# Batch 0's plain q and k loaded as fp32 over two other queues, half the warm-up matmuls, and the output in eleven tiles

## The chip, the core and the metric

One core of a Trainium2 chip runs the kernel. A core has TensorE (PE; its weight loads are shown as PEld), VectorE (DVE), ScalarE (ACT), GpSimd (POOL), a sync engine (SP) and 16 DMA engines. The metric is the device time of one execution in microseconds (us). A second number, the span, runs from the first to the last instruction in the profile of one execution; the time is a little longer than the span. DMAs are issued by SP, ACT or POOL, each through a queue of its own; here a DMA that casts fp32 to fp16 on its way is issued by POOL.

## The reference

The program is windowed attention followed by a soft mixture of experts:

```python
q, k, v: (8, 8, 576, 64) fp32                      # batch, heads, rows, width
scores = q @ k.T / 8
mask: heads 0-3 "plain":   0 <= i - j < 32
      heads 4-7 "dilated": 0 <= i - j < 128 and (i - j) % 4 == 0
x = softmax(masked scores) @ v                     # -> (4608, 512)
logits = x @ phi                                   # phi (512, 32): 8 experts x 4 slots
slot_input = softmax(logits, over rows).T @ x      # (32, 512)
slot_out[e] = relu(slot_input[e] @ w1[e]) @ w2[e]  # w1 (8, 512, 1024), w2 (8, 1024, 512)
out = softmax(logits, over slots) @ slot_out       # (4608, 512) fp32
```

The inputs are 28.3 MB of q, k and v and 33.6 MB of expert weights, all fp32; the output is 9.4 MB.

## The kernel before

**Homes.** SBUF holds eight tiles `home0` to `home7` (all line numbers below are those of the kernel before). `load_batch(b)` fills home b with the fp16 copies of batch b: `qp`, `kp` (plain heads 0 to 3, 96 partitions x 4 heads x 6 rows), `vp`, `vt` (v of the plain heads, and the last 64 rows of all heads), `qd`, `kd` (dilated heads) and `vd`. All are casting DMAs on POOL's queue, issued in program order at L160 (v), L182 (q and k) and, for batch 0 alone, L185. When a batch is used up, `load_w1` (L237) and `load_w2` (L248, L251) put the weights of expert b into the same home, again on POOL's queue. POOL's order is fixed by hand (`manual_schedule`): all 56 loads of the eight batches, then the 17 weight loads; each weight load waits until its home is free.

**Batch 0.** SP first loads heads 0 and 1 of q in fp32 into a tile of its own, `q0` (L76), and then the identity `ident` (L80), the band mask `mask` (L81) and `phi_sb` (L82). A DVE copy casts `q0` into home 0 (L179). POOL loads the plain k of batch 0 first (L182), then heads 2 and 3 of its q (L185), then v.

**Start of the engines.** DVE begins with 25 fills of constants (L104 to L131), ahead of the cast at L179. PE begins with `warm(6, ...)`: 24 matmuls of `ident` by itself (L549), whose result nothing reads, and then the transposes of unit 0.

**Attention.** A unit is one pair of heads of one batch; 32 units run in the order plain, dilated, plain, dilated within a batch. `transposes` (L273, L288) turns q and k on PE, with copies out at L278 and L293; `select_v` gathers rows of v with matmuls (L203, L214, L223), copied out by ACT at L211 and L232; `scores`, `softmax_parts`, `values` and `x_transposes` follow; `front_logits`, `front_rows` and `front_slots` do the mixture's first half one batch behind. `front_rows` also sums, for every output row, the slot weights, and keeps their reciprocals in `rrow`, one column for each set of 128 output rows (L469).

**Experts and output.** `expert_in` (L667, L675, L678) and `expert_out` (L691) run over the eight experts. The last weight load is that of `w2[7]`, in two halves (L251): the last eight matmuls at L691 need them. ACT copies the sum out as `so` (L708). The output loop then takes 18 tiles of 256 rows: two matmuls of 128 rows each (L729), one scaled out of PSUM by ACT (L731) and one by DVE (L733) into one of six buffers `ot`, and one DMA of 512 KB on SP's queue (L739). A partition holds two neighbouring rows, 4 KB that lie together in the output. Tile 0 is done in four half-width matmuls, and two DMAs of 256 KB (L737).

Of the kernel before, what the change touches and what calls it, by code (L numbers as in the profile page):

```python
# [9 lines left out]
FP32 = mybir.dt.float32  # L10
# [5 lines left out]
B = 8  # L16
H = 8
S = 576
D = 64
# [5 lines left out]
N_ROWS = B * S  # L25
DMODEL = H * D
# [6 lines left out]
QW = 160  # L33
RP, NP = 6, 96
RD, ND = 12, 48
CL = S // DIL
DW = CL + 16
NU = 4 * B
NV = 2

# [14 lines left out]
def kernel(  # L55
# [10 lines left out]
    nc = tc.nc  # L66
# [17 lines left out]
    keep = ctx.enter_context(tc.tile_pool(name="keep", bufs=1))  # L84

# [14 lines left out]
    phi4 = kept([128, 4, 4, N_SLOTS], "phi4")  # L100
    U_sb = kept([128, DMODEL], "U_sb", FP32)

    for b in range(1, B + 1):
        nc.vector.memset(ET[:, S * b : S * b + 64], 0.0)  # L104
    nc.vector.memset(quarter, 0.25)
    nc.vector.memset(quarters, 0.25)
    nc.vector.memset(ones, 1.0)
    nc.vector.memset(xT[:, :, S:], 0.0)
    nc.vector.memset(pick, 0.0)
    nc.vector.memset(phi_by, 0.0)  # L110

    Pp = kept([128, 2, NKB, 256], "Pp")
    P1 = kept([128, 2, 4, 128], "P1")
# [8 lines left out]
    nc.vector.memset(Pp[:, :, :, QW:], 0.0)  # L122

    nc.vector.memset(Pp[:, :, 4, 64:QW], 0.0)
    nc.vector.memset(Pp[0:1, :, 4, 64:128], 1.0)
    nc.vector.memset(P2, 0.0)
    nc.vector.memset(P2[0:1, :, :, 0, 16:32], 1.0)
    for i in range(2):
        nc.vector.memset(vd[i][:, :, D : D + 1], 1.0)
    for i in range(NV):  # L130
        nc.vector.memset(vp[i][:, :, :, D : D + 1], 1.0)  # L131

    hTp = [kept([128, 8, 60], f"hTp{e}") for e in range(4)]

# [13 lines left out]
    ps_s = tc.alloc_tile_pool(name="ps_s", bufs=2, space=bass.MemoryType.PSUM)  # L148

    raws, w_tiles = {}, {}  # L150

    def load_batch(b):
        t = homes[b]
        parts = {}
        at = 0

        def load_v(nm, h0, n_h, r0, dst):
            n_p = dst.shape[0]
            dst = dst.rearrange("p (h x) -> p h x", h=n_h)
# [99 lines left out]
    def transposes(u):  # L259
        b, hp = unit(u)  # L260
        for nm in ("q", "k"):
            if nm == "q":
                dst = qT_pool.tile([128, S], FP16, name=f"qT{u}", tag="qT")
                qTs[u] = dst
            else:
                dst = kTp if hp < 2 else kTd
                kTs[u] = dst
            if hp < 2:
                raw = raws[b][nm + "p"]
                rg = ring.tile([128, RP, NP], FP16, name=f"rg{nm}{u}", tag="ring")  # L270
                for r in range(RP):
                    for h in range(2):
                        nc.tensor.transpose(  # L273
                            rg[64 * h : 64 * h + 64, r, :],
                            raw[:, 2 * hp + h, D * r : D * r + D],
                            ident[0:NP, 0:NP],
                        )
                nc.scalar.copy(  # L278
                    out=dst[:, 0:S].rearrange("c (p r) -> c p r", r=RP),
                    in_=rg.rearrange("c r p -> c p r"),  # L280
                )
            else:
                raw = raws[b][nm + "d"]
                rg = ring.tile([128, 3, 4, ND], FP16, name=f"rg{nm}{u}", tag="ring")
                for a in range(3):
                    for cc in range(2):
                        j = 2 * a + cc
                        nc.tensor.transpose(  # L288
                            rg[:, a, 2 * cc : 2 * cc + 2, :].rearrange("c h p -> c (h p)"),
                            raw[:, hp - 2, 128 * j : 128 * j + 128],  # L290
                            ident[0:NP, 0:NP],
                        )
                (nc.scalar.copy if nm == "q" else nc.vector.tensor_copy)(  # L293
                    out=dst[:, 0:S].rearrange("c (g p a) -> c g p a", g=4, a=3),
                    in_=rg.rearrange("c a g p -> c g p a"),
                )

    def scores(u):
        b, hp = unit(u)
# [159 lines left out]

    def front_rows(b):  # L460
        r0 = b * S
        t0, t1 = r0 // 256, (r0 + S) // 256
# [4 lines left out]
        for n in range(2 * (t1 - t0)):  # L467
            c0 = 256 * t0 + 256 * (n // 2) + n % 2
            nc.tensor.matmul(  # L469
                ep[:, 10, n : n + 1], ET[:, c0 : c0 + 255 : 2], quarter, start=True, stop=True  # L470
            )
        nc.vector.reciprocal(out=rrow[:, 2 * t0 : 2 * t1], in_=ep[:, 10, 0 : 2 * (t1 - t0)])

    def front_slots(b):
        up = ring.tile([128, DMODEL], FP32, name=f"u{b}", tag="ring")
# [123 lines left out]
    select_v(0)  # L599
    st = scores(0)  # L600
    softmax_parts(0, st)
    transposes(2)
    for u in range(NU + 5):
# [9 lines left out]
        if 0 <= b < B:  # L613
            if ph == 1:
                if b == B - 1:
                    last_logits(lr, 3)
                    last_slots(last, lr)
                front_logits(b)
            elif ph == 2:
                front_rows(b)  # L620
            elif ph == 3 and b < B - 1:
                front_slots(b)
        if u == 1:
            spread_phi()
        if u == NU:
# [88 lines left out]

    ps_f = tc.alloc_tile_pool(name="ps_f", bufs=3, space=bass.MemoryType.PSUM)
    out_pool = ctx.enter_context(tc.tile_pool(name="outp", bufs=1))
    ots = [out_pool.tile([128, 2, DMODEL], FP32, name=f"ot{i}", tag=f"out{i}") for i in range(6)]
    for t in range(N_ROWS // 256):
        ot = ots[t % 6]
        rows = out[256 * t : 256 * t + 256, :].rearrange("(m j) d -> m j d", j=2)  # L720
        for j in range(2):
            cols = ET[:, 256 * t + j : 256 * t + j + 255 : 2]
            scale = rrow[:, 2 * t + j : 2 * t + j + 1]
            halves = ((0, 256), (256, 512)) if t == 0 else ((0, 512),)
            for n, (d0, d1) in enumerate(halves):
                n = j if t else n
                fp = ps_f.tile([128, DMODEL], FP32, name=f"f{t}_{j}{n}", tag=f"f{n}")
                fp = fp[:, 0 : d1 - d0]
                nc.tensor.matmul(fp, cols, so[:, d0:d1], start=True, stop=True)  # L729
# [6 lines left out]
            if t == 0:  # L736
                nc.sync.dma_start(out=rows[:, j], in_=ot[:, j])  # L737
        if t > 0:
            nc.sync.dma_start(  # L739
                out=rows.rearrange("m j d -> m (j d)"), in_=ot.rearrange("m j d -> m (j d)")  # L740
            )
    ps_f.release()

# [29 lines left out]
```

## Time and profile before

| what | before |
|---|---|
| time, median of 3 runs | 185.99 us (185.93 to 188.54) |
| time of the profiled execution | 186.0 us |
| its span | 184.2 us |
| busy: PE, DVE, ACT, POOL | 147.0, 117.1, 116.5, 48.3 us |
| read from HBM, written | 62.02 MB, 9.44 MB |
| POOL's queue: packets, MB written | 22480, 30.79 |
| SP's queue: packets, MB written | 3376, 9.89 |
| SP's first issues: `q0`, `ident`, `mask`, `phi_sb` | 0.74, 1.16, 1.65, 2.12 us |
| POOL's first issues: k, q, v | 1.29, 2.09, 2.73 us |
| warm-up matmuls | 24, from 4.05 us, 3.47 us |
| first output DMA issued | 158.72 us |

How to read it: the row of slices in the profile gives the busy share of each engine in 40 equal parts of the span. GB/s counts what DMA engines wrote, so a cast of fp32 to fp16 counts half of what it reads, and a plain fp32 copy counts all of it. The DMA share is packet time over the time of 16 engines; packets overlap, so it can be over 1. A table by stretch gives busy time of each engine, the granted clock of TensorE, the DMA share and the rate for any stretch of the span. The chain of waits follows back from the last instruction to what released each piece of work.

### The profile page before, as it was taken

What the parts mean: (1) busy time and instruction counts of PE and PEld (TensorE: products, weight loads), DVE (VectorE), ACT (ScalarE), POOL (GpSimd) and SP (SyncE); (2) the same over time, 40 slices, a digit from 0 to 9 for tenths busy, and PEclk for the clock granted to TensorE, in tenths of its full rate; (3) what the DMA queues carried; (4) which work ended last, traced back from release to release, by engine and by line L of the source; (5) the groups of instructions that cost most, each with busy time, mean ns of one, the idle gap of its engine ahead of it and who ended that gap; (6) DMA issues with size and microseconds to landing.
All of it is one profiled execution on the core that took longest, in us unless ns stands there. A gap on an engine that the chain in (4) does not pass through costs nothing.

```text
span 184.2 us, 6078 instructions
## 1 busy us (share of the span) xinstructions
PE 147.0 (80%) x2595; PEld 101.0 (55%) x2595; DVE 117.1 (64%) x363; ACT 116.5 (63%) x208; POOL 48.3 (26%) x77
## 2 busy tenths in 40 slices
PE   1879889699899899979978989989698983895300
PEld 1647666566676667757666667667585330331000
DVE  7605995948778788797786877869801110595610
ACT  2248879677888797798789698878131220785510
POOL 7754545455554545410011010022000000000000
PEclk9999999979999999999999999999965798589755
DMA  5999999999999999999999999999999994399995
GB/s 106 190 202 204 200 202 203 202 201 204 200 203 200 204 201 206 215 211 221 205 223 210 222 206 218 213 216 221 210 222 213 209 212 87 128 422 418 421 418 245
DMA packets 25883, 41.06 MB, mean 223 GB/s; under 512 B 1792, under 2 KB 20352, under 8 KB 24832
## 3 DMA queue, kind: packets, MB, share of 16 engines
q0 software_dynamic: 22480, 30.79, 94.4%
q1 hardware_dynamic: 3376, 9.89, 13.6%
q8 instruction: 20, 0.33, 0.6%
q14 instruction: 7, 0.06, 0.1%
HBM read 62.02 MB, written 9.44 MB: 388 GB/s over the span
## 4 chain that ended last, share of the span: by engine, by line
DMA 54%; PE 15%; issue 14%; ACT 5%; DVE 4%; POOL 4%; ACTq 0%; POOLq 0%
DMA home<-in_moe_w_dram 32%; DMA home<-in_q_dram 6%; DMA home<-in_k_dram 6%; DMA out_dram<-ot 5%; DMA home<-in_v_dram 5%; PE f L729 3%; PE l L434 2%; ACT pd L342 2%; PE sel L203 2%; PE rgx L414 1%; PE o L393 1%; PE rgq L273 1%; POOL home L182 1%; DVE P L351 1%; ACT qT L278 1%
## 5 line engine op out<-in xcount | busy, mean ns | idle before, releaser
L398 DVE TENSOR_TENSOR x<-o,rc 128x384 f16<-128x384 f32 x64 | 30.0, 482 | 0.5
L330 ACT ACTIVATE pr<-s 128x960 f16<-128x960 f32 (+1 forms) x32 | 24.8, 783 | 0.8 <-PE s L313 0.8
L342 ACT ACTIVATE pd<-s 128x640 f16<-128x640 f32 x32 | 21.0, 706 | 0.8 <-PE s L313 0.7
L160 POOL DMA_DIRECT2D home<-in_v_dram x24 | 16.6, 692 | 16.3 <-DMA home<-in_k_dram 9.6
L733 DVE TENSOR_SCALAR ot<-f,rrow 128x512 f32<-128x512 f32 (+1 forms) x19 | 13.3, 720 | 11.1 <-PE f L729 7.3
L203 PE MATMUL sel<-home,pick 32*128 32x256 f16 x128 | 16.8, 291 | 1.2 <-DMA home<-in_v_dram 0.7
L414 PE MATMUL rgx<-ident,x 128*128 128x128 f16 x160 | 14.6, 223 | 3.8 <-ACT qT L293 3.5
L333 DVE TENSOR_TENSOR Pp<-pr,mask 128x960 f16<-128x960 f16 (+2 forms) x48 | 16.4, 394 | 0.3 <-ACT pr L330 0.3
L731 ACT ACTIVATE ot<-f,rrow 128x512 f32<-128x512 f32 (+1 forms) x19 | 12.3, 665 | 6.8 <-DMA out_dram<-ot 4.3
L397 DVE RECIPROCAL rc<-o 128x6 f32<-128x6 f32 x64 | 10.0, 175 | 9.8 <-PE o L393 9.6
L278 ACT COPY qT<-rgq 128x576 f16<-128x576 f16 x16 | 10.3, 642 | 9.3 <-PE rgq L273 8.8
L420 ACT COPY xT<-rgx 128x512 f16<-128x512 f16 x16 | 9.7, 605 | 9.7 <-PE rgx L414 9.7
L729 PE MATMUL f<-so,ET 128*128 128x512 f16 (+1 forms) x38 | 12.3, 454 | 4.4 <-ACT ot L731 3.4
L237 POOL DMA_DIRECT2D home<-in_moe_w_dram x8 | 4.5, 565 | 37.6 <-PE rgq L288 30.1
L211 ACT CAST vp<-sel 128x512 f16<-128x512 f32 x16 | 9.4, 590 | 7.7 <-PE sel L203 7.0
L414 PEld LDWEIGHTS <-x 128*128 128x128 f16 x160 | 9.8, 98 | 7.4 <-issue 5.3
L273 PEld LDWEIGHTS <-home 96*64 96x64 f16 x384 | 11.1, 116 | 4.3 <-issue 2.4
L434 PE MATMUL l<-xT,phi 128*128 128x288 f16 x64 | 11.4, 318 | 2.2 <-ACT qT L278 2.0
L182 POOL DMA_DIRECT2D home<-in_k_dram x16 | 10.6, 662 | 9.4 <-DMA home<-in_q_dram 7.9
L293 DVE COPY kTd<-rgk 128x576 f16<-128x576 f16 x16 | 12.0, 751 | 0.4 <-PE rgk L288 0.4
L393 PE MATMUL o<-vp,Pp 128*128 128x65 f16 x288 | 12.0, 197 | 0.0
L293 ACT COPY qT<-rgq 128x576 f16<-128x576 f16 x16 | 10.4, 647 | 2.2 <-PE rgq L288 1.7
(106 smaller groups left out, 286.6 us busy)
## 6 DMA issues: line engine op xcount, KB each, us to landing
home<-in_moe_w_dram POOLq DMA_DIRECT2D x15, 1024.0 KB, 32.6
out_dram<-ot SPq DMA_DIRECT2D x17, 512.0 KB, 5.0
home<-in_k_dram POOLq DMA_DIRECT2D x16, 288.0 KB, 10.0
home<-in_q_dram POOLq DMA_DIRECT2D x15, 288.0 KB, 9.9
home<-in_v_dram POOLq DMA_DIRECT2D x16, 256.0 KB, 10.0
home<-in_moe_w_dram POOLq DMA_DIRECT2D x2, 512.0 KB, 30.3
home<-in_v_dram POOLq DMA_DIRECT2D x8, 64.0 KB, 8.8
out_dram<-ot SPq DMA_DIRECT2D x2, 256.0 KB, 2.1
```

The costliest lines, as they stand in the source:

```text
L160: nc.gpsimd.dma_start(out=dst, in_=v[b, h0 : h0 + n_h, r0 : r0 + 4 * n_p, :].rearrange("h (p r) d -> p h (r d)", r=4),)
L203: nc.tensor.matmul(sel[:, n, 0], pick[rows, r].rearrange("p i j -> p (i j)"), raw[rows, :, r, :], start=(r == 0), stop=(r == 3), tile_posi ...
L293: (nc.scalar.copy if nm == "q" else nc.vector.tensor_copy)(out=dst[:, 0:S].rearrange("c (g p a) -> c g p a", g=4, a=3), in_=rg.rearrange(" ...
L330: nc.scalar.activation(out=pr, in_=st[:, :, 0:n], func=AF.Exp, scale=SCALE)
L333: nc.vector.tensor_tensor(out=Pp[:, :, b0 : b0 + nb, 0:w], in0=pr[:, :, at : at + nb * w].rearrange("p h (t c) -> p h t c", c=w), in1=mask ...
L342: nc.scalar.activation(out=pr[:, part].rearrange("p c e t -> p e c t"), in_=st[:, :, 0 : 2 * DW].rearrange("p e (c t) -> p e c t", c=2), f ...
L393: nc.tensor.matmul(to, lhs, rhs, start=(n == 0), stop=(n == len(mms) - 1), skip_group_check=True)
L398: nc.vector.tensor_tensor(out=x[:, blocks[0] : blocks[0] + nb, D * hl : D * hl + 2 * D].rearrange("p t (h d) -> p t h d", h=2), in0=ot[:, ...
L414: nc.tensor.transpose(rg[:, 128 * blk : 128 * blk + 128], x[:, blk, hl : hl + 128], ident)
L434: nc.tensor.matmul(lp, phi4[:, kc].rearrange("p a s -> p (a s)"), xT[:, kc, 288 * c : 288 * c + 288], start=(kc == 0), stop=(kc == 3),)
L729: nc.tensor.matmul(fp, cols, so[:, d0:d1], start=True, stop=True)
L733: nc.vector.tensor_scalar(out=ot[:, j, d0:d1], in0=fp, scalar1=scale, scalar2=None, op0=ALU.mult)
```

## The change

1. *Batch 0's plain q and k.* The tile `q0` is gone, and so are POOL's loads of batch 0's plain k and of half its q. All four plain heads of q and k are copied in fp32 into home 7 (whose own data come much later), in two halves: heads 0 and 1 of k over ACT's queue, the other three pieces over SP's. SP's order is now `ident`, q heads 0 and 1, `mask`, q heads 2 and 3, k heads 2 and 3, `phi_sb`. DVE casts the two halves of q into home 0, ACT the two halves of k. POOL's first load is v.
2. *Warm-up.* 12 matmuls in place of 24.
3. *Fills.* DVE keeps three fills ahead of the first casts in program order; the others move behind the first transposes (`fill_pads`) or behind unit 0 (`fill_rest`). `select_v(0)` may not be placed ahead of the last transpose of unit 0.
4. *Output.* Eleven tiles: 256, 256, seven times 512, 256 and 256 rows, from four buffers twice as large. A partition of a large tile holds four neighbouring rows, 8 KB, and its DMA 1024 KB. `front_rows` lays out `rrow` to match; in the last batch it has 8 small matmuls in place of 6.

```diff
+OUT_TILES = [(0, 2), (256, 2)] + [(512 + 512 * i, 4) for i in range(7)] + [(4096, 2), (4352, 2)]
+OUT_COLS = [sum(nj for _, nj in OUT_TILES[:i]) for i in range(len(OUT_TILES))]
...
-    q0 = consts.tile([NP, 2, RP * D], FP32, name="q0")
-    nc.sync.dma_start(
-        out=q0,
-        in_=q[0, 0:2].rearrange("h s d -> (h s) d").rearrange("(g p r) d -> p g (r d)", g=2, r=RP),
-    )
     nc.sync.dma_start(out=ident, in_=ident_dram.ap())
-    nc.sync.dma_start(out=mask[:, 0 : QW + 64], in_=band_dram.ap())
-    nc.sync.dma_start(out=phi_sb, in_=moe_phi.rearrange("(p r) s -> p r s", r=4))
...
+    staged = {}
+    for i, ten in ((0, q), (1, k)):
+        at = homes[7][0:NP, 3072 * i : 3072 * i + 3072].bitcast(FP32).rearrange("p (g x) -> p g x", g=4)
+        of = ten[0, 0:4].rearrange("h s d -> (h s) d").rearrange("(g p r) d -> p g (r d)", g=4, r=RP)
+        staged["qk"[i]] = (at, of)
+    for half in range(2):
+        for nm, (at, of) in staged.items():
+            queue = nc.scalar if nm == "k" and half == 0 else nc.sync
+            queue.dma_start(out=at[:, 2 * half : 2 * half + 2], in_=of[:, 2 * half : 2 * half + 2])
+        if half == 0:
+            nc.sync.dma_start(out=mask[:, 0 : QW + 64], in_=band_dram.ap())
+    nc.sync.dma_start(out=phi_sb, in_=moe_phi.rearrange("(p r) s -> p r s", r=4))
+
+    def cast_first(half):
+        pair = slice(2 * half, 2 * half + 2)
+        nc.vector.tensor_copy(out=raws[0]["qp"][:, pair], in_=staged["q"][0][:, pair])
+        nc.scalar.copy(out=raws[0]["kp"][:, pair], in_=staged["k"][0][:, pair])
...
-            if b == 0 and nm == "qp":
-                nc.vector.tensor_copy(out=parts[nm][:, 0:2], in_=q0)
-                rest = (parts[nm][:, 2:4], src[:, 2:4])
-            else:
+            if b > 0 or hs > 0:
                 nc.gpsimd.dma_start(out=parts[nm], in_=src)
             if nm == "kp":
-                if b == 0:
-                    nc.gpsimd.dma_start(out=rest[0], in_=rest[1])
                 load_v("vp", 0, 4, 0, t[:, 6144:7168])
...
-    warm(6, ring, "ring")
+    warm(3, ring, "ring")
     ctx.enter_context(tc.manual_schedule(engines={mybir.EngineType.Pool}))
-    for b in range(B):
+    load_batch(0)
+    cast_first(0)
+    cast_first(1)
+    for b in range(1, B):
         load_batch(b)
     spread_constants()
-    transposes(0)
+    first = transposes(0)
+    fill_pads()
     spread_masks()
     spread_v(0)
     transposes(1)
-    select_v(0)
+    with tc.issue_after(first.ins):
+        select_v(0)
...
-    ots = [out_pool.tile([128, 2, DMODEL], FP32, name=f"ot{i}", tag=f"out{i}") for i in range(6)]
-    for t in range(N_ROWS // 256):
+    ots = [out_pool.tile([128, 4, DMODEL], FP32, name=f"ot{i}", tag=f"out{i}") for i in range(4)]
+    for i, (t0, nj) in enumerate(OUT_TILES):
...
-            cols = ET[:, 256 * t + j : 256 * t + j + 255 : 2]
+                nc.tensor.matmul(
+                    fp, ET[:, c0 : c0 + 127 * nj + 1 : nj], so[:, d0:d1], start=True, stop=True
+                )
```

More of the change, by code (lines that the diff above doesn't have):

```diff
@@ L101 @@
     U_sb = kept([128, DMODEL], "U_sb", FP32)
[L103 to L108, printed above, removed]
     nc.vector.memset(pick, 0.0)
-    nc.vector.memset(phi_by, 0.0)
     Pp = kept([128, 2, NKB, 256], "Pp")
@@ L121, with fill_pads, fill_rest @@
     nc.vector.memset(kTd[:, S:], 0.0)
[L122 to L131, printed above, removed]
+    def fill_pads():
+        nc.vector.memset(Pp[:, :, :, QW:], 0.0)
+        nc.vector.memset(Pp[:, :, 4, 64:QW], 0.0)
+        nc.vector.memset(Pp[0:1, :, 4, 64:128], 1.0)
+        nc.vector.memset(ones, 1.0)
+        for i in range(2):
+            nc.vector.memset(vd[i][:, :, D : D + 1], 1.0)
+        for i in range(NV):
+            nc.vector.memset(vp[i][:, :, :, D : D + 1], 1.0)
+        nc.vector.memset(P2, 0.0)
+        nc.vector.memset(P2[0:1, :, :, 0, 16:32], 1.0)
+    def fill_rest():
+        nc.vector.memset(phi_by, 0.0)
+        nc.vector.memset(xT[:, :, S:], 0.0)
+        nc.vector.memset(quarter, 0.25)
+        nc.vector.memset(quarters, 0.25)
+        for b in range(1, B + 1):
+            nc.vector.memset(ET[:, S * b : S * b + 64], 0.0)
     hTp = [kept([128, 8, 60], f"hTp{e}") for e in range(4)]
@@ L272, in transposes @@
                     for h in range(2):
-                        nc.tensor.transpose(
+                        done = nc.tensor.transpose(
                             rg[64 * h : 64 * h + 64, r, :],
@@ L287, in transposes @@
                         j = 2 * a + cc
-                        nc.tensor.transpose(
+                        done = nc.tensor.transpose(
                             rg[:, a, 2 * cc : 2 * cc + 2, :].rearrange("c h p -> c (h p)"),
@@ L296, in transposes @@
                 )
+        return done
     def scores(u):
@@ L461, in front_rows @@
         r0 = b * S
-        t0, t1 = r0 // 256, (r0 + S) // 256
+        cols = [
+            (n0 + j, t0 + j, nj)
+            for n0, (t0, nj) in zip(OUT_COLS, OUT_TILES)
+            if r0 < t0 + 128 * nj <= r0 + S
+            for j in range(nj)
+        ]
         ep = ring.tile([128, 11, N_SLOTS], FP32, name=f"e{b}", tag="ring")
@@ L466, in front_rows @@
             nc.vector.tensor_copy(out=Er[b % 2], in_=ep[:, 0:10])
-        for n in range(2 * (t1 - t0)):
-            c0 = 256 * t0 + 256 * (n // 2) + n % 2
+        for n, (_, c0, nj) in enumerate(cols):
             nc.tensor.matmul(
-                ep[:, 10, n : n + 1], ET[:, c0 : c0 + 255 : 2], quarter, start=True, stop=True
+                ep[:, 10, n : n + 1], ET[:, c0 : c0 + 127 * nj + 1 : nj], quarter, start=True, stop=True
             )
-        nc.vector.reciprocal(out=rrow[:, 2 * t0 : 2 * t1], in_=ep[:, 10, 0 : 2 * (t1 - t0)])
+        if cols:
+            n0 = cols[0][0]
+            nc.vector.reciprocal(out=rrow[:, n0 : n0 + len(cols)], in_=ep[:, 10, 0 : len(cols)])
     def front_slots(b):
@@ L622 @@
                 front_slots(b)
+        if u == 0:
+            fill_rest()
         if u == 1:
@@ L716 @@
     out_pool = ctx.enter_context(tc.tile_pool(name="outp", bufs=1))
-    ots = [out_pool.tile([128, 2, DMODEL], FP32, name=f"ot{i}", tag=f"out{i}") for i in range(6)]
-    for t in range(N_ROWS // 256):
-        ot = ots[t % 6]
-        rows = out[256 * t : 256 * t + 256, :].rearrange("(m j) d -> m j d", j=2)
-        for j in range(2):
-            cols = ET[:, 256 * t + j : 256 * t + j + 255 : 2]
-            scale = rrow[:, 2 * t + j : 2 * t + j + 1]
-            halves = ((0, 256), (256, 512)) if t == 0 else ((0, 512),)
-            for n, (d0, d1) in enumerate(halves):
[L726 to L729, printed above, removed]
+    ots = [out_pool.tile([128, 4, DMODEL], FP32, name=f"ot{i}", tag=f"out{i}") for i in range(4)]
+    for i, (t0, nj) in enumerate(OUT_TILES):
+        ot = ots[i % 4]
+        rows_out = out[t0 : t0 + 128 * nj, :].rearrange("(m j) d -> m j d", j=nj)
+        halves = ((0, 256), (256, 512)) if i == 0 else ((0, 512),)
+        for j in range(nj):
+            c0, scale = t0 + j, rrow[:, OUT_COLS[i] + j : OUT_COLS[i] + j + 1]
+            for n, (d0, d1) in enumerate(halves):
+                n = n if i == 0 else j % 2
+                fp = ps_f.tile([128, DMODEL], FP32, name=f"f{i}_{j}{n}", tag=f"f{n}")[:, 0 : d1 - d0]
+                nc.tensor.matmul(
+                    fp, ET[:, c0 : c0 + 127 * nj + 1 : nj], so[:, d0:d1], start=True, stop=True
+                )
                 if n == 0:
@@ L735 @@
                     )
-            if t == 0:
-                nc.sync.dma_start(out=rows[:, j], in_=ot[:, j])
-        if t > 0:
+            if i == 0:
+                nc.sync.dma_start(out=rows_out[:, j], in_=ot[:, j])
+        if i > 0:
             nc.sync.dma_start(
-                out=rows.rearrange("m j d -> m (j d)"), in_=ot.rearrange("m j d -> m (j d)")
+                out=rows_out.rearrange("m j d -> m (j d)"), in_=ot[:, 0:nj].rearrange("m j d -> m (j d)")
             )
```

## The prediction

> **What bounds the kernel now.** I read the row of slices first, then the chain of waits, then the two ends of the span in a table by stretch, and last who waited for whom.
>
> ```profile
> DMA  5999999999999999999999999999999994399995
> GB/s 106 190 202 204 200 202 203 202 201 204 200 203 200 204 201 206 215 211 221 205 223 210 222 206 218 213 216 221 210 222 213 209 212 87 128 422 418 421 418 245
> ```
>
> The DMA engines are at work in every slice but the first, two near 155 us and the last. The rate is flat at about 202 GB/s (404 GB/s read) while q, k and v are cast, about 215 with the weights, and 420 with the output. So the middle is one stream of bytes, and a faster engine there buys nothing. What can move is when the stream gets up to speed, the break near 155 us, and the output. The chain of waits says the same:
>
> ```profile
> 124.88 31.26 DMA home<-in_moe_w_dram
> 156.14 0.04 issue
> 156.19 0.64 PE sop L691 x4
> 156.83 0.02 issue
> 156.85 0.59 ACT so L708
> 157.44 0.04 issue
> 157.49 6.02 PE f L729 x18
> ```
>
> The last weights, issued at 124.88, land 31.26 us later, and only then can L691 end, `so` be copied and the output start. How far are the engines behind that landing? Among the waits of PE:
>
> ```profile
> PE sop L691 <- DMA home<-in_moe_w_dram: 3.2, 2, 2.1
> ```
>
> PE waits 3.2 us in two pieces for the two halves of `w2[7]`. With data at hand it would have been through 3.2 us earlier: that is the slack of all compute, and after 16 us PE waits for no other load. Now the head, and the first output transfers:
>
> ```profile
> 2.80:3.00 0.20, 0.00 (x0) 0.00 (x0) 0.20 (x2) 0.00 (x0) 0.20 (x1) 1.00 1.03 326
> 3.25:3.50 0.25, 0.00 (x0) 0.00 (x0) 0.24 (x4) 0.00 (x0) 0.25 (x1) 1.00 0.84 106
> 3.75:4.00 0.25, 0.00 (x0) 0.00 (x0) 0.16 (x2) 0.00 (x0) 0.25 (x1) 1.00 0.72 65
> 4.75:5.00 0.25, 0.25 (x4) 0.16 (x2) 0.00 (x0) 0.00 (x0) 0.25 (x1) 1.00 1.01 154
> 5.50:6.00 0.50, 0.50 (x4) 0.25 (x2) 0.35 (x3) 0.00 (x0) 0.50 (x1) 1.00 1.28 209
> ...
> 159.60:159.80 0.20, 0.20 (x2) 0.12 (x1) 0.20 (x1) 0.05 (x1) 0.00 (x0) 0.50 0.94 369
> 160.80:161.00 0.20, 0.20 (x2) 0.15 (x1) 0.19 (x1) 0.20 (x1) 0.00 (x0) 0.50 0.41 144
> 161.20:161.40 0.20, 0.20 (x2) 0.12 (x1) 0.20 (x1) 0.15 (x1) 0.00 (x0) 0.50 1.09 451
> ```
>
> The last three columns are the granted clock, the DMA share and GB/s written. `q0` and `ident` on SP's queue reach 326 GB/s at 2.9 us. Then they are done, and POOL's stream, first issued at 1.29, climbs only from 65 GB/s near 3.9 us to 209 near 5.7. That hollow is where the change can act.
>
> **The head.** Removed from POOL's queue: k of four heads (589,824 bytes) and q of two (294,912), together 884,736 bytes read, 442 KB written as fp16. Two POOL issues go with them, 0.81 and 0.66 us, so what follows is issued about 1.5 us sooner. Added: the same bytes in fp32 on SP's and ACT's queues, 1,180 KB there in place of `q0`'s 295. SP's order becomes `ident`, q, `mask`, q, k, `phi_sb`; at 0.42 to 0.44 us each (its rows) the last is issued near 3 us, and ACT's k can be issued near 0.75, ahead of ACT's table load. First data came 0.9 us after the first issue (0.74 to between 1.6 and 1.8), so these queues have bytes to move from 1.7 to past 5 us. What is missing there now: from 3.25 to 5.5 us the rows add up to 287 KB written, of which `mask` and `phi_sb` are 120 KB plain and 167 KB cast, 454 KB read in all; at 404 GB/s it could be 909 KB, so 455 KB are missing, 1.13 us. From 5.5 to 8 us the rate is 190 against 202, 0.15 us more. Sum 1.3 us, if the new traffic fills the hollow and the stream then runs as before. Bounds: if POOL's stream alone decides, it is shorter by 442 KB at 202 GB/s, 2.2 us. If the engines are in truth occupied in the hollow (a DMA share of 0.72 to 1.01 beside 1.3 in the steady part), nothing is filled, and the moved bytes cost 885 KB at 326 GB/s, 2.7 us, for the 2.2 they took: a loss of 0.5. I take 1.3, worked out from the hollow itself, with 2.2 and -0.5 as ends.
>
> The Trainium skill ("DMA: Bandwidth & Descriptors", Issuing engines are not separate DMA queues) speaks against any gain: DMAs from all issuing engines run on the same 16 engines and interleave, and issuing from several only saves issue time. By that rule the head would give what the second rival below gives; that 65 GB/s was moved where 404 were being read later speaks for room.
>
> **Casts, fills, warm-up.** Added: one more DVE cast (0.58 us, the row of `q0`) and two ACT casts of the same 96x768, between its rows of 0.64 us for 128x576 and 0.97 for 128x960, so some 2.2 us in all on two engines; ACT's second cast waits for the last piece on SP's queue and holds back the copies of `sel` behind it, DVE's second holds back the mask fills. Removed: 12 warm-up matmuls of 0.145 us each (3.47 us for 24), which ended at 7.5 us, when the first transposes began (7.45). With `ident` first on SP's queue and q behind it, transposes may begin near 5 us. All of it is hidden by the 3.2 us of slack at L691, and by the 2 us that the start is earlier; I cost it at nothing. If that cover were gone, its price is its excess over 3.2 us. The two extra matmuls in `front_rows` (0.1 us each) lie in the same cover.
>
> **The output.** Nothing changes up to the second tile. Its DMA is issued at 160.21, its bytes begin near 161.05 (the dip at 160.80 is the seam), 0.84 us later, and take 1.25 us at 420 GB/s: to 162.3. In that time the third tile must be ready. Now it needs two rounds of ACT and DVE; DVE's four runs from 159.39 last 3.31 us, 0.86 apart, so the large third tile is issued near 161.92 instead of 161.07, and its bytes begin near 162.75: a hole of 0.45 us. Its ends are 0 and one whole round, 0.86. After that a tile takes 2.5 us to write and 1.7 us at most to fill, with three in the queue, so there is no second hole; the last two tiles are of the old size, and the tail from 182.3 stays. DMAs of 1024 KB with runs of 8 KB may go faster than 4 KB at 419: the weights are read at 430 (215 written), which over seven tiles (17.5 us) would be 0.45 us; no faster at all is the other end, and a loss is not excluded, which I bound by the seam seen now at 160.80 (0.15 us short of full). I take a gain of 0.2.
>
> **Sum.** The profiled execution took 186.0 us, 184.2 of it span, and agrees with the median of 185.99. 186.0 - 1.3 + 0.45 - 0.2 = 184.95, that is 185.0 us, 0.5% less.
>
> **Rivals.**
> *POOL's stream decides alone.* Plain fp32 bytes run beside it without slowing it, and the head gives 2.2 us: 186.0 - 2.2 + 0.45 - 0.2 = 184.05. For it: the steady rate is so flat, at 202, that a limit of this queue is possible. Against it: 404 GB/s read is close to the 420 of the output on the other queue, so the engines look like the limit.
> *The engines are full in the head.* Nothing is filled, the fp32 bytes cost 0.5 us more: 186.0 + 0.5 + 0.45 - 0.2 = 186.75, slower than before. Place: 3 to 6 us; it decides when the share there counts work and not waiting. For it: the share of 0.72 to 1.01. Against it: 326 GB/s were written a moment before at 1.03.
> *TensorE stays slow and compute becomes the bound.* The granted clock is shown as full from the start, yet twelve transposes take 0.69 us until 16 us and 0.45 from 20 us on. If with half the chain everything from 7.5 to 20 us (PE busy 10.3 us) took twice as long, then less the 2.2 us idle there, the 3.2 us of slack and the 2 us of earlier start, 2.9 us would show: 185.0 + 2.9 = 187.9. Against it: those transposes ran at the slower pace even after the whole chain. The Trainium skill ("TensorE: Matmul & The Clock Gate", Part 1: The HAM clock gate) says that about 3.4 us of sustained work lifts the clock; by that rule the old chain of 3.47 us just reaches it and the new one alone doesn't, so this rival is its case, and the transposes that follow without a break speak for the lift coming soon after.
>
> **How the numbers follow.** The forecast 0.50, with a range of its own from 184.3 to 185.6 (a head of 0.9 to 1.9, the output between its ends); POOL's stream alone 0.24; full engines 0.16; slow TensorE 0.05; something unseen 0.05. Leaving out 2 in 10 gives 183.5 to 187.0. About 2% (3.7 us) is what a measurement of this kernel can tell from no change; none of the first three comes near, slow TensorE could in a worse form, and the unseen case may go either way: faster 0.05, same 0.91, slower 0.04.
>
> **What would show it.** Right: rates between 3.25 and 5.5 us above 300 GB/s in place of 65 to 190; the last weights land 1.3 us earlier (L691 near 154.9 in place of 156.19); PE still waits there for DMA; a stretch of 0.3 to 0.5 us at low rate about 5 us after L691's last matmuls; the output rate then 420 or a little more. Wrong: the weights land as late as before (full engines), or over 2 us sooner (POOL's stream); L691 no longer waits for DMA (compute is the bound); output stretches under 400 GB/s after the first hole.

## The result: about 1 us slower

Over 14 runs each the changed kernel's median was 187.28 us (185.86 to 188.02), the old one's 186.18 (185.92 to 188.54). The ratio is 1.0051, 95% interval [1.003, 1.0072]: some 0.9 us slower, clear of zero, but within the 2% that count as no change. The ratio, here and below, is taken over the fast runs alone and is not the quotient of the two medians. The forecast was 185.0 us in a range up to 187.0: the sign was wrong, and the time just outside. The profiled execution took 186.97 us, 185.2 of it span, against 186.0 and 184.2: 1.0 us more, so it can stand for the median.

### The profile page after: what moved, and what is told of

It is laid out like the page before. It is cut to its first block, busy times and chain, and to the rows that moved or that the text cites. A ratio compares the mean times of both kernels' runs of the same rounds, so it can differ in the third digit from the quotient of the medians.

```text
span 185.2 us, 6046 instructions
## 1 busy us (share of the span) xinstructions
PE 144.3 (78%) x2583; PEld 100.1 (54%) x2583; DVE 117.1 (63%) x364; ACT 117.1 (63%) x210; POOL 47.1 (25%) x75
## 4 chain that ended last, share of the span: by engine, by line
DMA 74%; issue 13%; PE 3%; ACT 2%; POOL 2%; DVE 1%; POOLq 0%; SPq 0%; DVEq 0%
DMA home<-in_moe_w_dram 33%; DMA home<-in_v_dram 15%; DMA home<-in_k_dram 11%; DMA home<-in_q_dram 11%; DMA out_dram<-ot 4%; PE f L751 3%; ACT ot L755 2%; DVE ot L757 1%; POOL home L258 1%; POOL home L247 1%; PE sop L715 0%; ACT so L732 0%; POOL home L261 0%; POOL home L175 0%; POOLq L258 0%
## 5 line engine op out<-in xcount | busy, mean ns | idle before, releaser
L757 DVE TENSOR_SCALAR ot<-f,rrow 128x512 f32<-128x512 f32 (+1 forms) x19 | 12.8, 719 | 12.7 <-PE f L751 7.5
L213 PE MATMUL sel<-home,pick 32*128 32x256 f16 x128 | 17.6, 290 | 3.7 <-DMA home<-in_v_dram 3.3
L755 ACT ACTIVATE ot<-f,rrow 128x512 f32<-128x512 f32 (+1 forms) x19 | 11.7, 665 | 7.2 <-DMA out_dram<-ot 5.4
L751 PE MATMUL f<-so,ET 128*128 128x512 f16 (+1 forms) x38 | 11.7, 438 | 3.9 <-ACT ot L755 3.0
L445 PE MATMUL l<-xT,phi 128*128 128x288 f16 x64 | 10.5, 299 | 1.9 <-ACT qT L288 1.7
L194 POOL DMA_DIRECT2D home<-in_k_dram x15 | 9.8, 654 | 8.4 <-DMA home<-in_q_dram 7.7
```

Source lines behind the costliest of these rows:

```text
L213: nc.tensor.matmul(sel[:, n, 0], pick[rows, r].rearrange("p i j -> p (i j)"), raw[rows, :, r, :], start=(r == 0), stop=(r == 3), tile_posi ...
L751: nc.tensor.matmul(fp, ET[:, c0 : c0 + 127 * nj + 1 : nj], so[:, d0:d1], start=True, stop=True)
L757: nc.vector.tensor_scalar(out=ot[:, j, d0:d1], in0=fp, scalar1=scale, scalar2=None, op0=ALU.mult)
```

## The profile after

I read it in the order of before. First the row of slices:

```profile
DMA  5999999999999999999999999999999993499995
GB/s 146 213 210 201 203 203 200 203 203 202 201 204 202 202 200 208 218 209 225 204 229 203 224 206 221 211 216 216 213 220 216 209 215 68 164 387 430 432 412 216
```

The middle is what it was. The first two slices hold more GB/s (146 and 213 for 106 and 190), which looks like the gain that was sought. But this row counts bytes written, and an fp32 piece writes 4 bytes where the casting stream writes 2. The end of the chain of waits:

```profile
124.36 32.24 DMA home<-in_moe_w_dram
156.61 0.04 issue
156.65 0.64 PE sop L715 x4
157.29 0.02 issue
157.32 0.59 ACT so L732
157.91 0.04 issue
157.95 4.01 PE f L751 x11
161.96 0.02 issue
161.99 0.51 ACT ot L755
```

The last weights were issued 0.52 us earlier (124.36 for 124.88) and landed 0.46 later: L715 begins at 156.65 in place of 156.19. It still waits for DMA, and longer than the 3.2 us of before:

```profile
PE sop L715 <- DMA home<-in_moe_w_dram: 3.9, 2, 2.0
```

So compute didn't become the bound: there is more slack than before, and less of the stream has been moved. In the table by stretch (last three columns: granted clock, DMA share, GB/s written) the hollow of the head looks filled at 3.3 us, and is back at 4.8 and 5.5, where the old kernel had written 154 and 209 and the new one writes 106 and 169:

```profile
3.25:3.50 0.25, 0.16 (x2) 0.17 (x3) 0.18 (x1) 0.00 (x0) 0.25 (x2) 1.00 1.09 313
3.75:4.00 0.25, 0.25 (x3) 0.16 (x2) 0.25 (x5) 0.00 (x0) 0.25 (x2) 1.00 0.77 193
4.75:5.00 0.25, 0.25 (x4) 0.13 (x2) 0.03 (x1) 0.25 (x1) 0.25 (x1) 1.00 1.07 106
5.50:6.00 0.50, 0.16 (x4) 0.17 (x6) 0.41 (x2) 0.00 (x0) 0.50 (x1) 1.00 0.99 169
```

The DMA issues say when the new pieces came (median us from issue to landing last):

```profile
home<-in_k_dram ACTq DMA_DIRECT2D x1, 288.0 KB, 3.6
home<-in_q_dram SPq DMA_DIRECT2D x2, 288.0 KB, 5.6
home<-in_k_dram SPq DMA_DIRECT2D x1, 288.0 KB, 8.9
phi_sb<-in_moe_phi_dram SPq DMA_DIRECT2D x1, 64.0 KB, 9.7
```

The third piece on SP's queue is k of heads 2 and 3, issued at 2.58 us. It takes 8.9 us, to 11.5; `phi_sb` behind it, 64 KB, takes 9.7. The forecast had these queues at work "to past 5 us"; they were at work to 12. The casting stream came later too. Its first load, v, was issued at 1.25 us where the old kernel issued v at 2.73, but POOL's first packet moved at 4.08 us, in the old kernel at 3.18.

Written bytes mislead where 4-byte and 2-byte streams mix. So the next table is worked out from the trace's DMA packets (queue, time and size of each), a casting packet counted with what it reads. "Plain" is SP's and ACT's queues, "POOL" the casting stream; rates in GB/s, and the KB of 3.5 to 8 us are 2 us of the one and 2.5 us of the other. The last column is when the last weight load was in on the mean of the 16 DMA engines, and on the slowest.

```
kernel            3.5-5.5 us       5.5-8 us         3.5-8, KB  by 14 us, KB  in: mean / slowest
                  plain+POOL       plain+POOL
before            24+212=236       13+352=365       1384       4186       154.24 / 155.80
after             106+88=194       135+178=313      1170       3946       154.56 / 156.30
e1_head_only      107+108=215      148+180=328      1250       4076       154.55 / 156.66
e3_mask_last      192+62=254       126+178=304      1268       4070       154.53 / 156.99
e5_late_pool      254+0=254        131+188=319      1306       3811       155.08 / 157.04
e13_v_first       30+176=206       8+350=358        1307       4045       154.45 / 156.28
e9_three_pieces   152+142=294      108+184=292      1318       4174       154.27 / 156.46
e10_two_queues    235+46=281       121+222=343      1420       4264       154.12 / 155.83
e11_v_later       114+200=314      128+196=324      1438       4071       154.36 / 156.10
e6_two_pieces     117+186=303      10+342=352       1486       4327       153.79 / 156.04
e4_no_fp32        12+300=312       0+368=368        1544       4102       154.27 / 156.18
```

Between 3.5 and 5.5 us plain traffic rose by 82 GB/s, and POOL's stream fell by 124. The hollow wasn't filled, it got deeper: 194 GB/s for 236, then 313 for 365. By 14 us the stream is 240 KB behind, 0.59 us at 404 GB/s. What is lost or won by then stays: by the same count of packets the changed kernel is still 188 KB behind at 150 us, `e5_late_pool` 375 at 14 us and 352 at 150, `e6_two_pieces` 141 ahead and then 205. And behind the landing of the last weights the kernels hardly differ: where the granted clock was at 0.50, the first output byte left 3.74 to 3.88 us after the slowest DMA engine was done, and the old tiles then took 23.2 to 23.4 us, whatever the head.

Whether the head is the cause, and which part of it, the runs had to tell. All ratios are against the old kernel, timed beside it on the same chip in 5 rounds; a ratio of 0.001 is 0.19 us.

## Experiments

**Which part.** The theory: the head costs the time. The rivals: the output's tiles, or the moved fills and shorter warm-up. `e1_head_only` is the changed kernel with the old 18 output tiles; `e2_out_only` the old kernel with the eleven.

> The head of the change (points 1 to 3) with the old output of 18 tiles. If the loss sits in the head (full engines: the fp32 bytes fill nothing), the last weights are used at 156.5 to 156.9 us as in the changed kernel, and the time is 0.3 to 0.7 us over the kernel before. If the head is neutral and all is the output's, the last weights are used near 156.2 and the time is that of before within 0.2 us.

> The old head with the output in eleven tiles. Theory of the hole: a stretch near 5.5 us after the last expert matmul at about half rate, some 0.45 us lost there, 0.25 us won back by the longer runs, and 0.2 to 0.5 us over the kernel before. If the output is neutral: within 0.1 us.

Measured: the head alone 187.36 us, ratio 1.0063 [1.0036, 1.009], 1.2 us slower; the output alone 185.93, ratio 0.9984 [0.9957, 1.001]. The loss is in the head, and larger than the 0.3 to 0.7 us expected of it. The tiles do not cost the 0.2 to 0.5 us that the theory of the hole gave; they may give 0.3 us back, with an interval that reaches zero. In the head-only kernel the last weights come still later:

```profile
157.01 0.62 PE L707 MATMUL sop<-home,hTp 128*32 128x512 f16 x4 [1.76 <-DMA home<-in_moe_w_dram]
```

`e7_fills_warm` puts only the fills and the warm-up into the old kernel:

```diff
...
-    warm(6, ring, "ring")
+    warm(3, ring, "ring")
...
-    transposes(0)
+    first = transposes(0)
+    fill_pads()
...
-    select_v(0)
+    with tc.issue_after(first.ins):
+        select_v(0)
...
+        if u == 0:
+            fill_rest()
```

> Points 2 and 3 alone: half the warm-up matmuls and the moved fills, with the loads and the output of the kernel before. If loads decide, no change within 0.2 us, with the last weights used near 156.2. If the fills or the colder TensorE cost time, up to the 1.2 us of the new head.

Measured: 186.41 us, 1.0006 [0.9977, 1.0034]. That leaves the loads.

**Is it the mask, late behind an fp32 piece?** `e3_mask_last` is `e1_head_only` with the mask put behind all of them, so that its short runs can't hold the pieces up:

```diff
-        if half == 0:
-            nc.sync.dma_start(out=mask[:, 0 : QW + 64], in_=band_dram.ap())
+    nc.sync.dma_start(out=mask[:, 0 : QW + 64], in_=band_dram.ap())
     nc.sync.dma_start(out=phi_sb, in_=moe_phi.rearrange("(p r) s -> p r s", r=4))
```

> The new head, old output, and on SP's queue the mask moved behind the three fp32 pieces. If packets of 448 bytes in the middle of that queue hold up the pieces behind them, the rates between 4 and 6 us rise from about 110 to 170 to above 250 GB/s and the last weights are used 0.5 us or more earlier than in the new head. If it is the start of POOL's stream that slows every queue, the low stretch stays and the last weights are used within 0.3 us of the new head.

Measured: 187.34 us, 1.0052 [1.0025, 1.008]. The pieces were in 1.5 us sooner (last fp32 packet 8.87 us for 10.38) and nothing was won: from 3.5 to 5.5 us plain traffic went up to 192 GB/s, POOL's down to 62, and the last weights were used at 157.35, for 157.01 in `e1_head_only`. This theory falls.

**Is any fp32 piece a loss?** `e4_no_fp32` takes `q0` out of the old kernel:

```diff
-    q0 = consts.tile([NP, 2, RP * D], FP32, name="q0")
...
-            if b == 0 and nm == "qp":
-                nc.vector.tensor_copy(out=parts[nm][:, 0:2], in_=q0)
-                rest = (parts[nm][:, 2:4], src[:, 2:4])
-            else:
-                nc.gpsimd.dma_start(out=parts[nm], in_=src)
+            nc.gpsimd.dma_start(out=parts[nm], in_=src)
```

> The kernel before, with heads 0 and 1 of q of batch 0 on POOL's queue too, so that no q or k goes in fp32. If POOL's stream alone decides, its 295 KB more cost 0.73 us: last weights used near 156.9. If the engines are full from the start, moving these bytes back costs nothing or wins up to 0.2 us. If what is free is only the time before POOL's first bytes land (1.7 to 3.3 us), that time is now empty and the cost is 0.5 to 0.7 us.

Measured: 186.39 us, 1.0013 [0.9984, 1.0043]: a single fp32 piece is worth nothing that can be told. Two pieces are `e6_two_pieces`, three `e9_three_pieces`, four `e1_head_only`; the rest of q and k goes to POOL's queue ahead of v.

```diff
         for nm, (at, of) in staged.items():
+            if half == 1:
+                continue
...
                 nc.gpsimd.dma_start(out=parts[nm], in_=src)
+            else:
+                nc.gpsimd.dma_start(out=parts[nm][:, 2:4], in_=src[:, 2:4])
...
-    cast_first(1)
```

> The new head with the old output, but only heads 0 and 1 of q and of k go in fp32 (one piece on SP's queue, one on ACT's); the other half comes over POOL's queue ahead of v. Interference grows with the fp32 bytes that meet POOL's stream: with 590 KB in place of 1180, most of it is through before POOL's first bytes at 3.3 us, and the time lies within 0.4 us of the kernel before, 0.7 us or more under the new head. If what costs is anything else in the new head (the fills, the casts, the warm-up), it stays near the new head, 1 us over before.

`e9_three_pieces` does the same for k alone (`if nm == "k" and half == 1`).

> The new head with the old output and three fp32 pieces in place of four: heads 2 and 3 of k come over POOL's queue, first there, then v. Theory of the dose: about 590 KB of fp32 fit ahead of POOL's first bytes, and each piece of 295 KB beyond that costs more on SP's queue (about 260 GB/s) than it takes from POOL's stream (404): two pieces took 185.8 us, four 187.4, so three take 186.3 to 186.9. Theory of the order: what costs is that POOL begins with v or that SP's queue carries a late k piece; then three pieces take 185.6 to 186.1.

Measured: two pieces 185.78 us, 0.998 [0.9955, 1.0004]; three 186.9, 1.0007 [0.9978, 1.0036]. By the ratios none, one, two and three all lie within 0.4 us of the old kernel, and the loss shows with the fourth. That isn't clean: the interval of three touches that of four, its median is 0.5 us over the 186.41 of the old kernel beside it and lies in the range that the theory of the dose gave (186.3 to 186.9), and with three pieces or two POOL begins with q or k, with four it begins with v. So a price per piece is not ruled out here.

**Does plain traffic disturb POOL's start?** `e5_late_pool` keeps POOL busy first:

```diff
+    nc.gpsimd.memset(homes[6][:, 0:4096], 0.0)
     load_batch(0)
```

> The new head with the old output, and a fill of 128x4096 fp16 on POOL ahead of its first load, so that POOL's stream begins some 2 to 4 us later. Theory of interference: beside a queue with fp32 pieces waiting, POOL's stream starts slowly and both queues crawl; alone, it came up in 1.5 us (the run without fp32). Then the fp32 pieces are through near 5.5 us at 330 to 380 GB/s, POOL's stream starts alone, no stretch of 4 us under 250 GB/s remains, and the last weights are used no later than in the new head (157.0), probably 0.3 to 0.6 us earlier, although POOL starts later. If the engines simply have a fixed amount of work from the start, or POOL's stream alone decides, the last weights are used later by the delay itself, 1 to 4 us.

Measured: 187.35 us, 1.0064 [1.004, 1.0087]. The first load on POOL went out 2.93 us later than at 1.25, and the loss is that of `e1_head_only`. Neither theory is met: the pieces were through at 7.4 us and not near 5.5, and the last weights were used at 157.42, 0.4 us after those of `e1_head_only` where the one theory had no delay and the other at least 1 us. In the medians, what POOL's stream moves early beside the pieces is worth next to nothing, though in the traces it comes to 265 KB by 14 us. The stretch in which the plain queues are alone:

```profile
0.73 3.51 POOL L601 MEMSET home<- 128x4096 f16 x1 [0.29 <-POOLq L774]
4.18 1.60 POOL L173 DMA_DIRECT2D home<-in_v_dram  x2
```

```profile
2.00:3.50 1.50, 0.26 (x3) 0.26 (x4) 0.28 (x1) 0.43 (x1) 1.50 (x1) 1.00 0.90 297
3.50:5.50 2.00, 1.56 (x12) 0.99 (x9) 1.58 (x12) 0.83 (x1) 2.00 (x3) 1.00 1.02 254
```

With no POOL stream beside them they make 297 and 254 GB/s, against the 404 the casting stream reads later, and the share is at 0.90 and 1.02. So a share near 1 is no sign of room here: the queues still had work waiting. Both queues together made 342 and 366 GB/s from 2.5 to 3.5 us; once ACT's piece was through, at 3.6, SP's queue made 227 to 286, with the mask's small packets among them until 5.

**Queue and order.** `e10_two_queues` sends both pieces of k over ACT's queue; `e11_v_later` keeps SP's order and puts batch 0's v, whose runs are the short ones, behind the dense q and k on POOL; `e15_both_cures` does both. Each starts from `e1_head_only`; the first two were timed on another chip than it, so they are compared by their ratios to the old kernel.

```diff
-            queue = nc.scalar if nm == "k" and half == 0 else nc.sync
+            queue = nc.scalar if nm == "k" else nc.sync
```

> The new head, old output, four fp32 pieces, but both pieces of k on ACT's queue. If SP's queue by itself is what is slow (230 to 290 GB/s once ACT's piece is through), two queues side by side stay above 330 GB/s until 5 us and the time falls by 0.5 us or more, to 186.8 or less. If the 16 engines are the limit, whichever queue feeds them, it stays within 0.3 us of the new head, 187.1 to 187.6.

```diff
-            if nm == "kp":
+            if nm == ("kp" if b > 0 else "kd"):
                 load_v("vp", 0, 4, 0, t[:, 6144:7168])
```

> The new head, old output, four fp32 pieces; on POOL's queue the dilated q and k of batch 0 go ahead of its three v loads, so that POOL's stream begins with runs of 1536 bytes written in place of 512. Theory of the dose: no change beyond 0.3 us from the new head, 187.1 to 187.6. Theory of the order (a start with short runs is what is slow): the stretch at 4 to 6 us goes above 250 GB/s, and the time falls to 186.8 or less.

> The new head, old output, with both cures: k on ACT's queue, and v behind the dilated q and k on POOL's. If each cure takes away the same collision, the two give what one gives, a ratio of 0.997 to 0.999. If they are separate losses, they add up: 0.994 or less.

Measured: two queues 186.29 us, 0.9982 [0.9955, 1.0009]; v later 186.64, 0.9986 [0.9959, 1.0012]; both 186.31, 1.0007 [0.999, 1.0023]. By the ratios either edit alone takes the loss away, and the two together don't add. The theories are met in time, not all in rate: two queues moved 281 GB/s from 3.5 to 5.5 us where above 330 was expected until 5; v later moved 314 where above 250 was. In the first, k's pieces and the last weights:

```profile
home<-in_k_dram ACTq DMA_DIRECT2D x2, 288.0 KB, 4.4
```

```profile
156.19 0.62 PE L707 MATMUL sop<-home,hTp 128*32 128x512 f16 x4 [1.96 <-DMA home<-in_moe_w_dram]
```

Both pieces of k are in 4.4 us after issue, for 3.6 and 8.9, and the weights are back at 156.19. In `e11_v_later` POOL's stream keeps 200 GB/s beside 114 plain, where `e1_head_only` had 108 beside 107. Its late piece of k took 9.3 us to land, longer than in `e1_head_only` (8.3), so it isn't that landing as such which costs. Is it v's early place alone?

`e13_v_first` is the old kernel with v first on POOL, which the change did too:

```diff
+        if b == 0:
+            load_v("vp", 0, 4, 0, t[:, 6144:7168])
+            load_v("vt", 0, 8, 512, t[96:112, 0:2048])
         for nm, ten, hs, rows in (
```

> The kernel before, with one thing changed: on POOL's queue v of the plain heads and the last rows go ahead of the plain k and q of batch 0. If beginning with v's short runs costs by itself, 0.5 us or more over before. If it costs only beside a long tail of fp32 pieces on SP's queue, no change within 0.3 us.

Measured: 186.46 us, 1.0013 [0.9986, 1.004]. Not by itself: in these runs the loss shows where v is first and three pieces are in a row on SP's queue, and with neither alone. `e14_after_two_queues` is the test on the whole changed kernel, with the one line of `e10_two_queues`:

> The whole changed kernel with the late piece of k on ACT's queue in place of SP's, one line. If SP's queue with three pieces beside POOL's start is the cause, the loss of 1 us is gone: at or under the kernel before (185.6 to 186.4 us, ratio 0.996 to 1.000). If the loss has another cause, 187 us as the changed kernel, ratio 1.005.

Measured: 186.23 us, 0.9995 [0.9969, 1.0021], against 1.0051 [1.003, 1.0072] for the changed kernel: one line is worth about 1 us.

**The output, and a better version.** `e8_out_four_small` puts two more small tiles ahead of the large ones, so that no large tile is awaited early:

```diff
+OUT_TILES = [(256 * i, 2) for i in range(4)] + [(1024 + 512 * i, 4) for i in range(6)] + [(4096, 2), (4352, 2)]
```

> The old head, and the output in twelve tiles: four of 256 rows, six of 512, two of 256, so that the first large tile comes when two more small ones are queued. Theory of the hole: the low stretch 5.5 us after the last expert matmul is gone and the gain of the longer runs stays, 0.25 to 0.4 us under the kernel before, and 0.2 to 0.4 us under the eleven tiles. If the hole costs nothing, it equals the eleven tiles.

Measured: 186.33 us, 1.0008 [0.998, 1.0035]: no gain that can be told. Its trace says why not: the hole did not go, it moved to the first large tile, the fifth, and the stores stood still for half a microsecond:

```profile
165.50:166.00 0.50, 0.47 (x2) 0.11 (x1) 0.50 (x2) 0.31 (x1) 0.00 (x0) 1.00 0.55 221
166.00:166.50 0.50, 0.13 (x2) 0.07 (x1) 0.50 (x2) 0.50 (x2) 0.00 (x0) 1.00 0.00 0
```

`e12_two_pieces_eleven` is `e6_two_pieces` with the eleven tiles:

> Two fp32 pieces with the output in eleven tiles. If head and output add up, the two small gains (0.4 and 0.25 us, each with an interval that reaches zero) give 185.4 to 185.7 us, under the kernel before with an interval clear of zero. If the output is worth nothing, 185.8.

Measured: 185.91 us beside 186.41, ratio 0.9958 [0.993, 0.9985]: 0.8 us faster than the old kernel by the ratio, 0.5 by the medians, with an interval clear of zero, and the lowest ratio of all that ran. It isn't clear of the intervals of its two parts, and 2% counts as no change here too; 185.4 to 185.7 us were expected. Its last weights:

```profile
155.70 0.62 PE L718 MATMUL sop<-home,hTp 128*32 128x512 f16 x4 [1.82 <-DMA home<-in_moe_w_dram]
```

## Why the forecast was wrong

*What bounds the kernel: right.* One stream of bytes up to the last weights, then the output. PE waited 3.9 us at L715 where 3.2 were the slack.

*The head: the step that failed*, "I take 1.3, worked out from the hollow itself", on the condition that "the new traffic fills the hollow and the stream then runs as before". It neither filled the hollow nor left the stream as it was. Measured: -1.2 us [-1.7, -0.7] from `e1_head_only` in place of +1.3, beyond even the lower end, -0.5. Two inputs were at fault, and two smaller ones in the sum. The shares of 0.72 to 1.01 were read as room, against the rival that named them, because 326 GB/s had been written a moment before; but that was one stretch of 0.2 us, and without POOL beside them the plain queues fell to 254 over 2 us (`e5_late_pool`). At that rate the moved 885 KB take 3.5 us for the 2.2 they took: a loss of 1.3, by the rival's own sum. That this is near the measured 1.2 is no proof, since kernels with the same bytes don't lose. And the issues were taken for the time at which bytes move: the last k piece, issued at 2.58, landed at 11.5, and POOL's first packet came 0.9 us later though v was issued 1.5 us sooner. In the sum, 120 KB of `mask` and `phi_sb` were put between 3.25 and 5.5 us; by the packets it was 65, so 508 KB were read, and the same reasoning would have given 1.0 us in place of 1.13. And the 65 GB/s held against 404 were written, not read: read, they are 126.

The rival "the engines are full" gave 186.75 and came nearest, with the right sign. As a rule it holds only in part: with the same fp32 bytes, `e10_two_queues`, `e11_v_later` and `e14_after_two_queues` show no loss. What the runs show in place of the filled hollow is that three fp32 pieces in a row on SP's queue and a POOL stream that starts with v cost about 1 us together. That they collide is the likely reading; `e5_late_pool`, which loses as much with POOL 2.9 us later, doesn't bear it out. The Trainium skill ("DMA: Bandwidth & Descriptors", Issuing engines are not separate DMA queues) says that DMAs from all engines interleave on the same 16 DMA engines, so that another queue saves issue time alone. That no arrangement of the loads alone came out clearly below the old kernel agrees. By it the 1.0063 [1.0036, 1.009] and 0.9982 [0.9955, 1.0009] of `e1_head_only` and `e10_two_queues` could differ by earlier issue alone: with ACT issuing both, k's second piece goes out by 1.62 us in place of 2.58. The 342 to 366 GB/s of both queues and the 227 to 286 of SP's in `e5_late_pool` speak for a second queue, the 326 of SP's queue alone in the old kernel against it. In `e10_two_queues` earlier issue and second queue came together; no run tells them apart.

*Open.* How 1.2 us come about. Between 3.5 and 8 us the changed kernel, `e1_head_only` and `e3_mask_last` moved least of all in the table, `e5_late_pool` next, which sorts the kernels that lose rightly but for `e13_v_first`, with 1307 KB and no loss. The size isn't explained: `e1_head_only`'s 134 KB less are only 0.33 us at 404 GB/s, and by 14 us `e11_v_later` and `e13_v_first` had moved no more than it and lost nothing. The last load's mean landing is 0.3 us later in the changed kernel, the slowest engine's 0.5. The rest may lie in how unevenly the 16 engines lag, 4.1 us from first to last in `e1_head_only` and 3.2 in the old kernel; but the slowest one's landing differs by 1.0 us between single profiles of kernels with the same loads (155.80 in before, 156.81 in `e8_out_four_small`), so one profile each can't show it.

*Casts, fills, warm-up at nothing: right.* `e7_fills_warm` is 1.0006 [0.9977, 1.0034]. Slow TensorE, the third rival, did not happen: the slack grew.

*The output: right in size, less so in its mechanism.* A hole of 0.45 us was forecast at the third tile. In the changed kernel two stretches run at 189 and 262 GB/s; against the 418 of before they lack 0.27 + 0.19 = 0.46 us:

```profile
162.50:163.00 0.50, 0.50 (x4) 0.25 (x3) 0.50 (x2) 0.50 (x2) 0.00 (x0) 1.00 0.48 189
163.00:163.50 0.50, 0.50 (x3) 0.17 (x2) 0.50 (x1) 0.50 (x2) 0.00 (x0) 1.00 0.61 262
166.00:170.00 4.00, 2.27 (x9) 0.79 (x8) 2.91 (x5) 2.45 (x4) 0.00 (x0) 1.00 1.03 434
```

The 434 GB/s of the last row are one stretch; from 180 to 182 us it is 399. Between 4.2 and 8.4 MB of output, where no hole falls, the packets give 427 GB/s with runs of 8 KB and 419 with 4 KB: 2%, some 0.35 us over seven tiles where 0.2 was taken. From the first to the last byte of output the changed kernel took 23.47 us, the old one 23.27: in this execution hole and gain nearly cancel. The hole isn't always as deep. In `e14_after_two_queues`, with the same tiles, the clock (third from last) is granted in full from 159 us, while in the changed kernel it was 0.50 or 0.56 up to 162, and the stores keep up:

```profile
159.00:160.00 1.00, 1.00 (x4) 0.34 (x3) 1.00 (x3) 1.00 (x3) 0.00 (x0) 1.00 0.88 338
161.50:162.00 0.50, 0.50 (x3) 0.17 (x2) 0.50 (x2) 0.50 (x2) 0.00 (x0) 1.00 0.99 410
162.00:162.50 0.50, 0.50 (x2) 0.17 (x2) 0.50 (x1) 0.50 (x2) 0.00 (x0) 1.00 1.24 524
```

```profile
161.00:162.00 1.00, 1.00 (x4) 0.34 (x3) 0.90 (x2) 0.70 (x2) 0.00 (x0) 0.56 0.93 373
```

The first fence is of `e14_after_two_queues`, the second of the changed kernel. In `e14_after_two_queues` the output takes 22.79 us from first to last byte, half a microsecond less than with the old tiles. In `e12_two_pieces_eleven` it takes 22.75, but with part of the hole (344 and 336 GB/s from 160 to 162 us) and a tail 0.4 us shorter. A slow clock doesn't explain every hole: that of `e8_out_four_small` lies where the clock is granted in full. What decides its depth is open; the forecast's ends, 0 and 0.86 us, hold all that was seen.

## What to carry to other kernels

A dip in bytes per second isn't room: look at the DMA share beside it, count a casting stream by what it reads, and price the new traffic by the rate that its own form reaches for as long as it will run, not by its best fifth of a microsecond. When loads are moved to another queue, their order and their neighbours can decide more than their bytes: here 295 KB on ACT's queue, issued 1 us earlier, instead of third on SP's was worth 1 us. And test the parts by themselves: the better output and the worse head had been put into one change, and two pieces with eleven tiles make 0.9958 [0.993, 0.9985] of the old time.

## What the runs showed of the hardware

Plain fp32 loads (1536-byte packets on 96 partitions), with no POOL stream beside them, ran at 342 to 366 GB/s while SP's and ACT's queues both had some, and at 254 over the next 2 us, when SP's alone had (`e5_late_pool`). A packet took 65 ns at the median before POOL's stream began and 78 beside it (the changed kernel, from 4.5 us on). Casting packets took 135 ns for 3072 bytes read, but overlap, at shares up to 1.33, and read 404 GB/s: moving bytes off the casting queue was no gain in rate here. Beside three pieces on SP's queue POOL's first packet moved at 4.08 us, without them at 3.18, though both kernels issued it near 1.3. A 64 KB load behind the pieces in SP's queue took 9.7 us to land. The 16 engines finish the same last load 3.0 to 4.2 us apart after 150 us of stream. With the clock granted in full the first output byte left 3.3 us after the last weights were in (`e14_after_two_queues`), at 0.50 of it 3.74 to 3.88. Stores in runs of 8 KB made 427 GB/s where nothing held them up, in runs of 4 KB 419.
